# A spectral mixing kernel with a gated projection behind it: the first entry's opening regrouped, and loads, first steps and last steps reordered

## The chip, the core and the metric

The kernel runs on one core of a Trainium2 chip. The metric is the device time of one launch in microseconds, taken over several runs, of which the median is given. The engines of the core are named as the profile names them: PE (matmul; PEld is its weight load), DVE (vector), ACT (scalar activation), POOL (general purpose) and SP (which here only issues DMAs). SP, ACT and POOL each feed a queue of DMAs, and the same 16 DMA engines serve all of them.

## What is computed

`x` holds 8 entries of 3136 positions and 256 channels. Each entry goes through a real FFT along its positions, a product with a complex filter, and the inverse FFT. The 25088 rows that come out pass a projection to 1024 columns, a softmax times its input (SoLU), a layer norm and a projection back to 256 columns.

```python
X = np.fft.rfft(x, axis=1)
y = np.fft.irfft(X * (filt_r + 1j * filt_i)[None], n=3136, axis=1)   # per entry
h = y.reshape(-1, 256) @ w_in                                        # 25088 x 1024
e = np.exp(h - h.max(-1, keepdims=True))
solu = h * e / (e.sum(-1, keepdims=True) + 1e-9)
ln = (solu - mean) / np.sqrt(var + 1e-6) * g_ln
out = ln @ w_out                                                     # 25088 x 256
```

## The kernel before

The FFT of 3136 points is split as 49 times 64. A **first step** does the 49-point part: a matmul over the positions that are 64 apart. It uses that the input is real, and that position n and position 63 - n of a row of 64 can share a matmul (`N1` = 49, `N2` = 64, `NH` = 32, `NS` = 25 frequencies kept of the 49). A **spectrum** stage does the 64-point part (`forward`, L304), multiplies with the filter (`multiply`, L313), and does the 64-point inverse (`inverse`, L329), in 7 units of up to two pairs of frequencies (`NP` = 13 pairs, `self.units`, L194). A **last step** (`back`, L389 for entry 0, `back_halves`, L361 for the others) does the 49-point inverse and leaves `y`, channels on partitions, as the stationary operand for the projection.

Between the steps the data must change its partition axis, and before this change every entry does that through DRAM: the first step's rows are stored to `d1` and fetched as `t2`, the spectrum's rows are stored to `d2` and fetched as `t4`.

**The opening** (L402 to L604) is written out by hand for entry 0, and each engine and queue runs its part in that order. It loads `x` in eight pieces of four positions (`fetch_x`, L504: one half on SP's queue, the mirrored half on POOL's), runs eight times two matmuls with the table `wf_t` as stationary operand (L226), copies them out on ACT (L228), and stores them to `d1` (L230) or, for the first 16 positions, copies them from SBUF to SBUF (L559). Rows of warming matmuls (`idle`, L532) fill PE's waits. The tables of the spectrum (`load_tables`, L465) come on POOL's queue and, for the last five pairs, on SP's. After the spectrum, eight fetches of two DMAs each (`fetch_first_back`, L347: 96 rows and 4 rows, in pairs) bring `t4`, 14 warming matmuls fill the round trip, and 16 groups of four matmuls write `y`. The projection weights arrive as 64-bit floats, eight pieces of 512 KB (`load_words`, L409, on POOL's queue), and are converted by DVE, ACT and POOL (`load_float64`, L416). The order of the conversions is `convert(0)`, `(1)` before the spectrum and `(2)` to `(7)` behind it. `fetch_second` (L460) brings six of the eight pieces of entry 1's `x` on SP's queue.

**The steps.** The rest is one loop over 196 blocks of 128 rows and 9 steps that drain it (`step`, L948). Two blocks form a pair with 7 matmul products for the first projection (`product`, L715) and 7 for the second (`project`, L834), which runs four pairs behind. A step also carries pieces of the next entries' transforms; `PLAN` (L37) says in which step each piece runs. Lists by step (`top`, `early`, `middle`, `late`, `stores`, `loads`, `spectrum_loads`) hold these jobs. For entry 1 the spectrum's units run from step 4 on, and their fetches (L915) are issued on SP's queue at the end of the step two before. In the last steps `regroup` (L790) turns blocks by eight SP DMAs, `deviations` (L802) and `regroup_deviations` (L812) send the layer norm's factors through DRAM with one and four SP DMAs, and `store_out` (L863) stores the result with two.

A matmul of 32-bit floats appears in the trace as two records. Up to eight DMAs that SP and ACT issued are under way at a time: a ninth waits until the eighth before it has landed.

Of the kernel before, what the change touches and what calls it, by code (L numbers as in the profile page):

```python
# [49 lines left out]
def dft_tables():  # L50
# [39 lines left out]
    return wf.reshape(NR, NK).astype(f32), wq.reshape(P, 2, 64).astype(f32), \  # L90
# [4 lines left out]
def kernel(  # L95
# [11 lines left out]
    wf_host, wq_host, wi_host, wb_host, de_host = dft_tables()  # L107
# [76 lines left out]
    class Spectrum:  # L184
# [5 lines left out]
        def __init__(self, e, pools, load, load_de):  # L190
            self.e, self.pools = e, pools
            self.load, self.load_de = load, load_de
            self.spare = {}
            self.units = [(i, min(2, NP - i)) for i in range(0, NP, 2)]  # L194
# [117 lines left out]

        def multiply(self, i, part, add=nc.vector.tensor_tensor):  # L313
# [15 lines left out]
        def inverse(self, i, pss):  # L329
            de, prods = self.des.pop(i), self.prods.pop(i)  # L330
            for r in range(2):
                for u in range(self.shape(i)[0]):
                    rows = slice(NQ * u, NQ * u + NQ)
                    self.product(i, pss[u][NQ * r:NQ * r + NQ], lambda v: de[rows, v, 1, r, :],
                                 prods[r][rows])
# [11 lines left out]
    def fetch_first_back(ch):  # L347
        by_16((nc.sync.dma_start, nc.sync.dma_start), t4s[0, ch],
              d2[0].rearrange("s (a n) c -> (s a) n c", a=4)[:, NCH * ch:NCH * ch + NCH, :])
# [52 lines left out]
    with ExitStack() as st:  # L402
        fpool = pool("fp", 1, stack=st)
        pools = {name: pool(name + "0", bufs, stack=st)
                 for name, bufs in (("r", 1), ("t2", 1), ("p", 2), ("g", 2))}
# [3 lines left out]
        def load_words(src, n):  # L409
            raw = wpool.tile([P, 512, 2], I32, name=f"raw_{n}", tag="raw")  # L410
            nc.gpsimd.dma_start(
# [48 lines left out]
        def fetch_second():  # L460
            for i in range(6):
                second.fetch_x(i, [lambda out, in_: nc.sync.dma_start(out=out, in_=in_)] * 2,
                               spare_piece(i))

        def load_tables(i0, n, dma):  # L465
            de = fpool.tile([P, n, 2, 2, NQ], FP32, name=f"de_{i0}", tag=f"de{i0}")
            dma(out=de, in_=de_dram[i0:i0 + n].rearrange("i p k u q -> p i (k u q)"))
            f = fpool.tile([P, n, 2, C], FP32, name=f"f_{i0}", tag=f"f{i0}")
# [26 lines left out]
        def begin(j):  # L495
            raws[j] = load_words(weights[j][1], j)

# [4 lines left out]
        rows_x = pools["r"].tile([P, NH, C], FP32, name="x_0", tag="r")  # L502

        def fetch_x(h, n0, n, r0, rows, dma):  # L504

            first, step = (n0, C) if h == 0 else (N2 - 1 - n0, -C)
            dma(out=rows_x[N1 * h + r0:N1 * h + r0 + rows, n0:n0 + n],
                in_=bass.AP(tensor=x.tensor, offset=x[0].offset + r0 * N2 * C + first * C,
                            ap=[[N2 * C, rows], [step, n], [1, C]]))

        st.enter_context(tc.manual_schedule())
        nc.sync.dma_start(out=wf_t, in_=wf_dram)
        pieces = NH // NCH

        fetch_x(0, 0, NCH, 0, N1 - 1, nc.sync.dma_start)
        fetch_x(0, 0, NH, N1 - 1, 1, nc.sync.dma_start)
        for i in range(pieces):
            if i:
                fetch_x(0, NCH * i, NCH, 0, N1 - 1, nc.sync.dma_start)
            fetch_x(1, NCH * i, NCH, 0, N1, nc.gpsimd.dma_start)  # L520
            if i in (4, 7):
                begin(i // 7)
        load_tables(0, 4, nc.gpsimd.dma_start)
        load_tables(4, 4, nc.gpsimd.dma_start)
        for i in range(pieces):
            sp.xs[i] = rows_x[:, NCH * i:NCH * i + NCH]

            sp.first(i, (0, 1), ps_h.tile([P, 2, 512], FP32, name=f"pa_0_{i}", tag="h"),
                     nc.scalar.copy, sp.xs[i][0:NK])
            sp.store_first(i, 0, lambda out, in_: by_16((nc.scalar.dma_start, nc.sync.dma_start), out, in_))  # L530
# [10 lines left out]
        idle_row(8, "idle")  # L541
# [5 lines left out]
        for j in range(2):  # L547
            convert(j)
# [51 lines left out]
        for j in (5, 6, 7):  # L600
            convert(j)
# [483 lines left out]
```

## Time and profile before

| | |
|---|---|
| time, median of 3 runs | 1637.28 us (1636.35 to 1648.25) |
| the profiled execution | 1626.78 us, its span 1624.9 us |
| PE busy | 1550.2 us, 95% of the span |
| PEld busy | 1047.4 us, 64% |
| DVE busy | 1305.4 us, 80% |
| POOL busy | 1163.8 us, 72% |
| ACT busy | 902.8 us, 56% |
| DMA moved | 312.13 MB, mean 192 GB/s |
| queue q1 (SP) | 306260 packets, 169.81 MB, 40.7% of 16 engines |
| mean granted PE clock | 0.989 |

Busy shares are means over stages with different limits. In the middle of the kernel PE hardly ever stops; what happens in the first 215 us and in the last 45 us has to be read from those stretches by themselves. The profiled execution is 10.5 us below the median of the three runs, which were other launches; a sum made in the profile is a difference that is then set against the median.

### The profile page before, as it was taken

Reading aid. Unit: us, or ns where it says so; the run is one execution under the profiler, and the core shown is the slowest. Engines: PE = TensorE matmul, PEld = TensorE weight load, DVE = VectorE, ACT = ScalarE, POOL = GpSimd, SP = SyncE. Lnnn points to the kernel's source line nnn. Section 1 sums busy time; section 2 is a strip of 40 time slices with the busy share of each in tenths; the row PEclk is TensorE's granted clock in tenths of the full one; section 3 lists DMA queues with packets and bytes.
Section 4 is the critical chain, followed back from the end, with each engine's and each line's share of the span. In section 5 each row is a group of like instructions: output and inputs, shape, how many; then the busy total and the mean of one; then the engine's idle time right before and its main releaser. Section 6 shows DMA issues by size and latency. Waiting matters only on the chain.

```text
span 1624.9 us, 36998 instructions
## 1 busy us (share of the span) xinstructions
PE 1550.2 (95%) x12710; PEld 1047.4 (64%) x12710; DVE 1305.4 (80%) x2630; ACT 902.8 (56%) x1772; POOL 1163.8 (72%) x1328
## 2 busy tenths in 40 slices
PE   5798889999999999999999999999999999999997
PEld 2353356666766677666766676666777777777766
DVE  1686777998889989888999779887888777777772
ACT  2144455466565656566656655565556666665662
POOL 4445887778777877697688867788667767677774
PEclk8999899999999999999999999999999999999999
DMA  9888778877788778866787677866885554444443
GB/s 270 241 267 258 224 198 238 228 197 200 203 240 235 202 189 248 231 191 170 215 249 203 186 179 213 241 175 161 225 231 152 126 136 121 104 111 105 109 109 101
DMA packets 377805, 312.13 MB, mean 192 GB/s; under 512 B 63322, under 2 KB 343395, under 8 KB 377619
## 3 DMA queue, kind: packets, MB, share of 16 engines
q1 hardware_dynamic: 306260, 169.81, 40.7%
q0 software_dynamic: 34464, 101.68, 20.8%
q10 hardware_dynamic: 36896, 38.28, 7.9%
q8 instruction: 103, 1.69, 0.5%
q14 instruction: 82, 0.67, 0.1%
HBM read 124.86 MB, written 81.50 MB: 127 GB/s over the span
## 4 chain that ended last, share of the span: by engine, by line
PE 42%; DMA 3%; DVE 2%; issue 1%; POOL 1%; SPq 1%; ACT 0%; DVEq 0%; POOLq 0%; ACTq 0%
PE o L844 20%; PE m L723 18%; PE py L372 1%; PE pa L269 1%; PE pc L301 1%; PE pb L301 1%; DMA solu_t<-turn 1%; DMA out_dram<-ot 0%; DMA x<-in_x_dram 0%; DMA t<-d 0%; POOL u L702 0%; DMA rows<-rs 0%; DVE h L771 0%; DVE h L747 0%; SPq L816 0%
## 5 line engine op out<-in xcount | busy, mean ns | idle before, releaser
L844 PEld LDWEIGHTS o<-w_out_sb,solu_t 128*128 128x128 f32 x3136 | 381.6, 192 | 48.7 <-issue 43.0
L844 PE MATMUL o<-w_out_sb,solu_t 128*128 128x128 f32 x3136 | 400.9, 276 | 2.9 <-DVE ot L860 2.5
L723 PE MATMUL m<-w_in_sb,s 128*128 128x512 f32 x784 | 398.2, 609 | 5.1 <-DVE rsum L766 3.3
L844 PEld LDWEIGHTS o<-w_out_sb,u 128*128 128x128 f32 x2352 | 308.0, 192 | 146.4 <-issue 105.2
L844 PE MATMUL o<-w_out_sb,u 128*128 128x128 f32 x2352 | 312.0, 276 | 9.2 <-ACT ot L856 8.6
L723 PE MATMUL m<-w_in_sb,y 128*128 128x512 f32 x588 | 308.8, 608 | 8.5 <-DVE nmax L747 5.5
L771 DVE SCALAR_TENSOR_TENSOR h<-e,rsum,h 128x1024 f32<-128x1024 f32 x196 | 302.9, 1546 | 6.9
L733 ACT COPY h<-m 128x512 f32<-128x512 f32 x294 | 172.9, 588 | 241.0 <-PE m L723 217.1
L702 POOL TENSOR_TENSOR u<-solu_t 128x512 f32<-128x512 f32 x98 | 133.4, 1362 | 228.0 <-DMA solu_t<-turn 140.0
L856 ACT ACTIVATE ot<-o,rs_t 128x128 f32<-128x128 f32 x392 | 143.5, 366 | 261.1 <-PE o L844 240.1
L779 ACT ACTIVATE h<-h,nmu 128x1024 f32<-128x1024 f32 x196 | 225.0, 1148 | 51.9 <-DVE turn L787 51.4
L787 DVE STREAM_TRANSPOSE turn<-h 128x1024 f32<-128x1024 f32 x196 | 243.1, 1240 | 3.2
L747 DVE CUSTOM_DVE_ANT_0 h<-m,h 128x512 f32<-128x512 f32 x196 | 133.8, 683 | 132.3 <-ACT h L733 92.8
L755 ACT ACTIVATE e<-h,nmax 128x1024 f32<-128x1024 f32 x196 | 225.1, 1148 | 12.1 <-DVE h L771 11.8
L702 POOL TENSOR_TENSOR u<-solu_t,u 128x512 f32<-128x512 f32 x98 | 150.9, 1540 | 91.2 <-PE o L844 87.2
L723 PEld LDWEIGHTS m<-w_in_sb,s 128*128 128x128 f32 x784 | 128.8, 192 | 93.4 <-issue 84.0
L723 PEld LDWEIGHTS m<-w_in_sb,y 128*128 128x128 f32 x588 | 95.7, 191 | 108.4 <-issue 50.3
L860 DVE SCALAR_TENSOR_TENSOR ot<-o,rs_t,ot 128x128 f32<-128x128 f32 x294 | 101.9, 347 | 78.0 <-ACT ot L856 59.2
L702 POOL TENSOR_TENSOR u<-u,solu_t 128x512 f32<-128x512 f32 x98 | 162.4, 1657 | 0.9
L702 POOL TENSOR_TENSOR solu_t<-solu_t,solu_t 128x512 f32<-128x512 f32 x98 | 153.1, 1562 | 7.7
L702 POOL TENSOR_TENSOR s<-y 128x128 f32<-128x128 f32 x196 | 100.8, 514 | 0.4
L372 PEld LDWEIGHTS py<-wb_t,t 50*64 50x64 f32 x3584 | 58.0, 135 | 43.7 <-issue 22.0
(114 smaller groups left out, 1956.0 us busy)
## 6 DMA issues: line engine op xcount, KB each, us to landing
solu_t<-turn SPq DMA_DIRECT2D x784, 128.0 KB
out_dram<-ot SPq DMA_DIRECT2D x196, 128.0 KB
t<-d POOLq DMA_DIRECT2D x112, 200.0 KB, 6.2
d<-x POOLq DMA_DIRECT2D x100, 200.0 KB, 5.3
f<-f_dram POOLq DMA_DIRECT2D x39, 512.0 KB, 6.9
d<-g POOLq DMA_DIRECT2D x39, 512.0 KB, 4.8
t<-d ACTq DMA_DIRECT2D x36, 512.0 KB
x<-in_x_dram SPq DMA_DIRECT2D x112, 98.0 KB
```

Of the source, the lines that this page charges most:

```text
L372: nc.tensor.matmul(out=views[g][64 * h:64 * h + 64, cb, i, :], lhsT=t4[rows, i, c0:c0 + 64], rhs=wb_t[rows, 0:N1], start=True, stop=True)
L702: nc.gpsimd.tensor_tensor(out=out, in0=in0, in1=in1, op=op)
L723: nc.tensor.matmul(out=ms[j, bank], lhsT=lhsT, rhs=w_in_sb[:, w, :], start=m in (1, 2, 7), stop=True, skip_group_check=True)
L733: nc.scalar.copy(out=h_half(k, i), in_=ms[j, 0])
L747: nc.vector.tensor_tensor_reduce(out=h_half(k, i), in0=ms[j, bank], in1=h_half(*kept), scale=1.0, scalar=sofar, op0=ALU.add, op1=ALU.min, ...
L755: nc.scalar.activation(out=e, in_=hs[k], func=AFT.Exp, bias=nmaxs.pop(k)[:, 1:2], scale=-1.0, accum_out=esum)
L771: nc.vector.scalar_tensor_tensor(out=solu, in0=e, scalar=rsum, in1=solu, op0=ALU.mult, op1=ALU.mult, accum_out=nmu)
L779: nc.scalar.activation(out=solu, in_=solu, func=AFT.Square, bias=nmu, scale=-float(DFF), accum_out=variances[g][:, i:i + 1])
L787: nc.vector.transpose(out=turns[g][:, :, i, :], in_=solus[k].rearrange("p (f j) -> p f j", j=32))
L844: nc.tensor.matmul(out=pos[p, bank], lhsT=lhs[:, f, :], rhs=w[:, f, :], start=f == 0 and m in (1, 2, 7), stop=True, skip_group_check=True)
L856: nc.scalar.activation(out=out_half(p, *to)[0], in_=pos[p, 0], func=AFT.Copy, scale=rs)
L860: nc.vector.scalar_tensor_tensor(out=ot, in0=pos[p, bank], scalar=rs, in1=out_half(p, *kept)[0], op0=ALU.mult, op1=ALU.add)
```

## The change

It does this:

- Entry 0's `x` is loaded in two channel halves on two groups of 49 partitions (512-byte rows) on SP's and ACT's queues. Positions n and 63 - n are added and subtracted on DVE and POOL into `sums_x`, which lies in `y`. Then `sums_x` is the stationary operand: for each of 128 channels, two halves and two parts, a matmul of 49 by 64 by 25 with the small table `wx_t`, in seven groups of up to 20 channels, each copied out by ACT into `rows_x` with positions on partitions. `d1` and `t2` are not used for entry 0, nor are the SBUF-to-SBUF copies.
- `forward_whole` takes the place of `forward` for entry 0: matmuls over 128 partitions with a table (`de0`) half as large again.
- The tables come on SP's queue behind `x`. Weight pieces 0 to 3 stay on POOL's queue, 4 to 7 go to SP's, behind the fetches of `t4`. `convert(2)` moves ahead of the spectrum, `convert(3)` right behind it.
- Both sums of `multiply` run on POOL for entry 0 (one did before), and the warming matmul in each unit goes.
- `fetch_first_back` issues all eight 96-row parts, then all eight 4-row parts.
- Entry 1's spectrum fetches for steps 8, 10 and 12 move to ACT's queue and to the middle of the step two before.
- One part of the output weights' preparation moves from step 3 to step 2.
- In step 196 the exponential comes behind a projection and its copy. In step 198 the last group's factors go on POOL's queue at once.

```diff
-    def fetch_first_back(ch):
-        by_16((nc.sync.dma_start, nc.sync.dma_start), t4s[0, ch],
-              d2[0].rearrange("s (a n) c -> (s a) n c", a=4)[:, NCH * ch:NCH * ch + NCH, :])
+    def fetch_first_back(ch, part):
+        rows = (slice(0, 96), slice(96, NK))[part]
+        nc.sync.dma_start(out=t4s[0, ch][rows], in_=d2[0].rearrange("s (a n) c -> (s a) n c", a=4)[
+            rows, NCH * ch:NCH * ch + NCH, :])
...
+        def forward_whole(self, i, pss):
+            de, i0 = self.des[i], self.units[i][0]
+            for v in range(self.units[i][1]):
+                for r in range(2):
+                    for u in range(self.shape(i)[0]):
+                        nc.tensor.matmul(out=pss[r][NQ * u:NQ * u + NQ, v, :], lhsT=de[:, v, r, u, :],
+                                         rhs=self.turned[:, 2 * (i0 + v) + u, :], start=True, stop=True)
...
+        for i in range(4):
+            (nc.vector, nc.gpsimd)[i % 2].memset(x_q[32:64, :, quarter * i:quarter * i + quarter, :], 0.0)
+        for i in range(4):
+            for h in range(2):
+                fetch_x(0, h, quarter * i, quarter, 0, N1 - 1, nc.sync.dma_start)
+                fetch_x(1, h, quarter * i, quarter, 0, N1 - 1, nc.scalar.dma_start)
+            if i == 0:
+                for h in range(2):
+                    fetch_x(0, h, 0, NH, N1 - 1, 1, nc.sync.dma_start)
+                    fetch_x(1, h, 0, NH, N1 - 1, 1, nc.scalar.dma_start)
...
+        for i0, n in ((0, 4), (4, 4), (8, NP - 8)):
+            load_tables(i0, n, nc.sync.dma_start)
...
+        for i in range(4):
+            mirror(i, 0, nc.vector)
+            mirror(i, 1, nc.gpsimd if i % 2 else nc.vector)
+            if i == 1:
+                begin(0)
+            if i == 3:
+                for n in range(8):
+                    nc.tensor.matmul(out=ps_t.tile([P, 512], FP32, name=f"warm_{n}", tag="t"),
+                                     lhsT=sums_x[both, :, 0, 16], rhs=sums_x[both, 0:64, 0, 16:24],
+                                     start=True, stop=True)
+                for j in (1, 2, 3):
+                    begin(j)
+        for c0 in range(0, P, 20):
+            n = min(20, P - c0)
+            ps = ps_h.tile([P, 2, 512], FP32, name=f"pa_0_{c0}", tag="h")
+            for k in range(n):
+                for g in range(2):
+                    for part in range(2):
+                        rows = slice(64 * g, 64 * g + N1)
+                        nc.tensor.matmul(
+                            out=ps[64 * part:64 * part + 64, g, NS * k:NS * k + NS],
+                            lhsT=sums_x[rows, c0 + k, :, :].rearrange("p j m -> p (j m)"),
+                            rhs=wx_t[rows, part, 0:NS], start=True, stop=True)
+            nc.scalar.copy(
+                out=rows_x[:, 0:NS, :].rearrange("p s (g c) -> p g s c", g=2)[:, :, :, c0:c0 + n],
+                in_=ps[:, :, 0:NS * n].rearrange("p g (k s) -> p g s k", s=NS))
+            nc.tensor.matmul(out=ps_t.tile([P, 512], FP32, name=f"keep_{c0}", tag="t"),
+                             lhsT=sums_x[both, :, 0, 16], rhs=sums_x[both, 0:64, 0, 16:24],
+                             start=True, stop=True)
...
-            sp.multiply(i, 0, nc.vector.tensor_tensor)
+            sp.multiply(i, 0, nc.gpsimd.tensor_tensor)
             sp.multiply(i, 1, nc.gpsimd.tensor_tensor)
...
-            idle(pss[0])
...
-        for ch in range(pieces):
-            fetch_first_back(ch)
-        fetch_second()
+        for part in range(2):
+            for ch in range(pieces):
+                fetch_first_back(ch, part)
+        for j in (4, 5):
+            begin(j, nc.sync.dma_start)
+        fetch_second(0, 3)
+        for j in (6, 7):
+            begin(j, nc.sync.dma_start)
+        fetch_second(3, 6)
...
-            dma = nc.sync.dma_start if e == 1 else nc.scalar.dma_start
-            fetches = ahead(t, 2) if e == 1 else spectrum_loads[t - 2]
+            dma = nc.sync.dma_start if e == 1 and t < 8 else nc.scalar.dma_start
+            fetches = ahead(t, 2) if e == 1 and t < 8 else spectrum_loads[t - 2]
...
-            if 2 <= k < blocks + 2:
+            if 2 <= k < blocks:
                 exponential(k - 2)
             if proj:
                 project(p, 5)
                 keep_out(p, 1, (0, 1))
+            if blocks <= k < blocks + 2:
+                exponential(k - 2)
...
+            if j - 3 == pairs - 2:
+                deviations(j - 3, nc.gpsimd.dma_start)
             if 0 <= j - 4 < pairs:
                 project_sums(j - 4, 1)
-            if 0 <= j - 3 < pairs:
-                deviations(j - 3)
+            if j - 3 == pairs - 2:
+                regroup_deviations((j - 3) // 2, nc.gpsimd.dma_start)
+            elif 0 <= j - 3 < pairs:
+                deviations(j - 3, nc.sync.dma_start)
...
-        if k in (0, 1, 3, 4, 5, 6, 7):
-            prepare_w_out(k - (k > 2))
+        if k in (0, 1, 2, 4, 5, 6, 7):
+            prepare_w_out(k - (k > 3))
```

## The prediction

> **What bounds the kernel now.** I read the page's slices, then the busy time by stage. The columns are the stage, its length, then busy time (instructions) of PE, PEld, DVE, ACT and POOL, the granted clock, the DMA share and GB/s.
>
> ```profile
> core 0: us, PE busy (x) PEld busy (x) DVE busy (x) ACT busy (x) POOL busy (x), PEclk, DMA share, GB/s
> 0.00:10.00 10.00, 0.04 (x1) 0.04 (x1) 0.06 (x1) 0.03 (x1) 6.30 (x12) 1.00 0.80 167
> 10.00:29.00 19.00, 17.26 (x32) 6.24 (x32) 7.38 (x16) 9.35 (x9) 6.91 (x12) 1.00 1.04 317
> 29.00:50.00 21.00, 13.15 (x39) 5.21 (x43) 0.20 (x1) 1.19 (x2) 10.04 (x13) 0.76 0.89 227
> 50.00:80.00 30.00, 22.84 (x198) 10.68 (x189) 24.15 (x40) 6.44 (x12) 14.15 (x16) 0.89 0.90 265
> 80.00:92.20 12.20, 12.20 (x30) 5.43 (x29) 11.86 (x17) 1.63 (x3) 6.09 (x5) 1.00 0.80 240
> 92.20:106.50 14.30, 14.30 (x130) 14.28 (x128) 13.96 (x24) 7.29 (x15) 3.07 (x2) 1.00 0.81 227
> 106.50:133.50 27.00, 24.49 (x81) 10.72 (x80) 12.65 (x35) 11.60 (x20) 16.11 (x27) 1.00 0.85 298
> 133.50:215.00 81.50, 65.51 (x341) 28.61 (x340) 63.09 (x116) 39.94 (x73) 59.42 (x66) 0.90 0.80 235
> 215.00:1580.00 1365.00, 1349.61 (x11625) 937.24 (x11624) 1158.44 (x2354) 811.75 (x1609) 1020.41 (x1161) 1.00 0.69 186
> 1580.00:1625.00 45.00, 30.83 (x255) 28.94 (x253) 13.58 (x31) 13.58 (x31) 21.29 (x17) 0.99 0.40 104
> ```
>
> From 215 to 1580 us PE is 99% busy and the change leaves that work alone. It can gain only ahead of 106.5 us (the opening, until the first product), in the next 108 us (18 us without PE work), and in the last 45. The opening is a chain: first step until 29, the turn through DRAM until 50, spectrum until 79.9 (end of the last inverse), store and fetch until 92.2 under warming matmuls, last step until 106.5. DMA is near full through all of it.
>
> The timeline of PE shows the shape that the change multiplies, a burst of the later entries' last step, 50 rows, 64 columns loaded, 49 moved:
>
> ```profile
> 256.53 1.08 PE L372 MATMUL py<-wb_t,t 50*64 50x49 f32 x58 [0.37 <-DMA t<-d]
> 257.40 0.39 PE L301 MATMUL pb<-t,de 64*64 64x256 f32 x1
> 257.41 0.25 PE L372 MATMUL py<-wb_t,t 50*64 50x49 f32 x2
> ```
>
> 58 records start in 0.88 us, 15.2 ns each, four quarters of the array in turn.
>
> SP's timeline shows how `t4` arrives; the first of these fetches started at 86.62, and eight went out by 89.66:
>
> ```profile
> 91.33 0.30 SPq L181 DMA_DIRECT2D t<-d  x1
> 93.86 0.30 SPq L181 DMA_DIRECT2D t<-d  x1
> 95.47 0.30 SPq L181 DMA_DIRECT2D t<-d  x1
> 97.04 0.30 SPq L181 DMA_DIRECT2D t<-d  x1
> ```
>
> Each of these waits until the 96-row fetch four pairs earlier has landed: 4.7 us after the first issue, then 2.5, 1.6, 1.6 us apart, in order of issue. From the waits of PE between 106 and 215 us, the two longest:
>
> ```profile
> PE pb L301 <- DMA y<-d: 3.9, 1, 3.9
> PE pb L301 <- DMA x<-in_x_dram: 2.9, 1, 2.9
> ```
>
> They stand at 206.6 and 184.7 us, before the forward steps of entry 1 whose fetches SP issued only at 198.6 and 174.7, behind eight regrouping DMAs. The chain of waits at the end, at SP:
>
> ```profile
> 1600.37 1.88 SPq L816 DMA_DIRECT2D rs_t<-rows  x4
> 1602.35 5.36 SPq L799 DMA_DIRECT2D solu_t<-turn  x8
> ```
>
> **x.** 6272 rows of 512 B, 3.2 MB, and 0.5 MB of weights beside them. By the first stage's row 1.67 MB move in 10 us; the other 2.0 MB take 6.5 to 9 us at 317 to 227 GB/s, so 16.5 to 19. Packets are shorter now: SP's queue averages 40.7% x 16 x 1624.9 / 306260 = 34.5 ns for 554 B, ACT's 55.7 ns for 1037 B. 6272 of them on 16 engines are 13.5 or 21.8 us, so 16 to 24.3 from a start at 2.5. I take 18.5, near SP's row, whose packets are mostly this size. The memsets hold SP's half until about 3 us (2048 elements; a 128-element one took 0.17 us), its single rows until 5.5; ACT's half covers that. Without the cover: 3 us.
>
> **Mirrors.** DVE's sum of 512 elements starts every 0.61 us, POOL's takes 1.27. Behind the last quarter lie one of 1024 on each: POOL's 2.5 counts. All sums at 21.
>
> **Warming.** 16 records took 10.4 us from cold (34 to 45 us, clock 0.70). They start at 15.5, if they wait for their own quarter, or at 21: end 26 to 31.4. I take 28.5.
>
> **First step.** 512 matmuls, 1024 records x 15.2 ns = 15.6 us, plus seven warming pairs at 2 x 0.44 = 6.1 us: 50.2. The seven ACT copies (1000 elements; 1024 took 1.01) lie beside PE but the last, 0.5. The array may be kept less busy by 25 columns moved in place of 49: from 12 us (loads half hidden) to 34.6 us (each load's 135 ns over four quarters); I keep the row. [...]
>
> **Spectrum.** First forward: 16 records, two column halves, 0.215 each, 1.9 us: multiply starts at 52.6 (before: 50.15). Per unit DVE has four operations instead of five (4 x 0.61 = 2.4), POOL two sums (2.7 with gaps), PE forward 1.95 and inverse 1.1: 3.1, PE is next. 1.3 + 6 x 3.1 + 1.6 for the half unit, and 1 of the 2.6 us that POOL spends on four table DMAs: 22.5. Last inverse at 75.1 against 79.9: -4.8. The stage before held a wait of 4.8 us for `y<-d`; it is gone. If column halves do not overlap, forward costs 3.4, a unit 4.5: +8.4. The missing warming pair is covered as PE has 3.1 of every 3.1 us.
>
> **Turn and last step.** Store to fetch was 6.7 us with weights on the queues; a 128 KB store on POOL's queue lands in 3.2 us, plus 1.7 for copy and issue: 5, fetches from 80.1. Now the eight 96-row parts go first. Part 4 of a piece waits for its own piece's counter and then stands behind seven large ones, and every matmul needs both. Landings came in order of issue, so PE starts when all 3.15 MB are there. At 1.6 us each: 2 + 12.8 = 14.8 us; at the second stage's 317 GB/s: 2 + 9.9 = 11.9. If the small parts overtake, 4.6. I take 11.9, as eight large ones are now in flight with no weights beside them: start at 92.0, before 92.2. [...] PE idles 4.6 us behind its warming row and starts slower; the cold row above lost 3.5 us on 16 records (10.4 against 6.9): I take 2. First product at 108.3: **+1.8 us**.
>
> **Weights and entry 1.** SP's queue behind `t4` carries 2.1 MB of weights and 1.2 MB of `x`: at 240 GB/s the last weights land some 14 us behind `t4`, at 106, and two conversions of 4.6 us (eight DVE rows of 0.42 to 0.69) follow the last two: DVE is free near 114, before 113.3. Steps 0 and 1 (106.5 to 133.5) are PE's: 24.5 of 27 us, DVE 12.65, so 14 us of idle DVE cover it. Cover gone: 3 us. Filter stores, fetches and `convert` stand in the same order otherwise: 0.
>
> **Steps 2 to 14.** ACT issues the two late fetches some 9 us sooner, ahead of SP's regrouping. ACT may stand until a counter is free, with its copies and exponentials behind; entries 2 to 7 do so already. 6.9 us of PE wait go; DVE (63 of 81.5) and POOL's sums are next, so not all: 0 to -6.9, I take **-4.8**. The weight step from step 3 to 2: 2.5 us of DVE into idle time, 0 (± 1).
>
> **End.** SP loses four issues, 1.88 us, on the chain. POOL takes five (0.55 each) and waits for the first to land, ahead of its sums for pair 96; those were waited for from 1599.7. The exponential frees the PE copy 1.2 us sooner (PE stood 2.36 us there). 0 to -3.1: **-2.5**.
>
> Sum: 1.8 - 4.8 - 2.5 = -5.5: 1626.78 becomes 1621.3, and against the median 1637.3 - 5.5 = 1631.8.
>
> **Rivals.** *The opening does what it could* (0.20): warming starts at 15.5, small parts overtake, so PE starts behind its warming row: last inverse 72.6, last step 84.9, first product at 99.2, -7.3; with -6.9 and -3.1: 1620. For it: two moves of 3.28 MB gone, 0.85 MB of larger tables added, 5.7 MB less at 227 to 317 GB/s. Against: landings in order. *The small matmuls do not overlap* (0.12, of which 0.10 past the point below): each record then pays for its load; at 34 ns +19 us, 1651, at 135 ns +123 us. It is slower by over 1% beyond 15.2 + (16.4 + 5.5) / 1.024 = 36.6 ns. Against: the burst above. *The later gains do not come* (0.18): DVE and POOL bind in steps 4 to 14, POOL waits for its factors in the end: 1639, and 1642 with `t4` at 1.6 us. Forecast: 0.50.
>
> 1% is 16.4 us, about what a measurement can tell. Faster needs all of the first rival: 0.15. Slower needs the second: 0.10. Within: 0.75. Low end 1617 (first rival, 12 us first step), high end 1648 (`t4` at 1.6 us, `x` at 24.3, nothing later).
>
> **What would show it.** Sums at 21 and first-step records 15 ns apart; last inverse near 75; PE standing before `py` until the eighth large fetch has landed, near 92; first product near 108; no wait before entry 1's forward at steps 8 and 10; the last regrouping 2 us sooner. An `x` that lands past 24, a unit over 4 us, or `py` beginning right behind the warming row would each make it wrong.

## The result, and the profile after

The changed kernel takes 1686.16 us (median of 4 runs, 1683.59 to 1687.36) where the kernel before takes 1637.82 (median of 4, 1636.35 to 1648.25): ratio 1.0276, 95% interval 1.0237 to 1.0314 (the two medians by themselves give 1.0295). The forecast was about 1632, within 1% of no change. The profiled execution is the fastest of the four, 1683.59 us, span 1681.8 against 1624.9 before: 56.9 us more.

The stages of the changed kernel, cut where its own work changes (same columns as before: stage, length, busy time and instructions of PE, PEld, DVE, ACT and POOL, granted clock, DMA share, GB/s):

```profile
core 0: us, PE busy (x) PEld busy (x) DVE busy (x) ACT busy (x) POOL busy (x), PEclk, DMA share, GB/s
...
29.00:70.70 41.70, 36.94 (x1037) 28.42 (x1036) 4.62 (x10) 7.24 (x7) 0.00 (x0) 0.60 0.45 130
70.70:80.70 10.00, 8.49 (x55) 4.31 (x50) 7.19 (x7) 2.15 (x4) 6.96 (x5) 0.79 0.00 0
80.70:103.20 22.50, 18.13 (x152) 9.83 (x152) 18.29 (x33) 6.44 (x12) 20.30 (x19) 0.85 0.37 123
103.20:120.70 17.50, 12.31 (x31) 5.28 (x29) 5.03 (x9) 1.06 (x2) 2.58 (x2) 0.96 0.81 225
120.70:148.10 27.40, 27.40 (x129) 27.40 (x129) 2.65 (x6) 7.29 (x15) 0.00 (x0) 0.50 0.78 260
148.10:243.40 95.30, 69.71 (x300) 27.51 (x300) 70.69 (x139) 41.18 (x72) 60.90 (x77) 0.91 0.63 182
243.40:1632.20 1388.80, 1367.64 (x11730) 947.87 (x11729) 1170.89 (x2380) 822.62 (x1628) 1041.86 (x1178) 1.00 0.69 187
1632.20:1681.80 49.60, 34.74 (x266) 32.16 (x264) 16.10 (x34) 13.84 (x31) 24.87 (x23) 0.94 0.37 96
```

The rows are the first step, the way to the first spectral product, the spectrum, the fetch of the last step's rows, the last step, the steps until the first matmul of the second projection, the middle, and the end. The loss is ahead of the middle: the first projection product starts at 148.1 us (106.5 before, +41.6), and the second projection 95.3 us behind it (86.0 before, +9.3). The middle and the end are 3.0 us longer each. The clock column shows what the sum priced at nothing in the first step and at 2 us in the last: 0.60 in the first step, 0.50 for the whole last step, where PE is busy in every microsecond.

PE's timeline in the first step (start, duration, line, operation, shape, number of records; in brackets the idle time before and what ended it):

```profile
28.99 2.53 PE L588 MATMUL pa<-wx_t,y 49*64 49x25 f32 x160
31.45 1.24 PE L595 MATMUL keep<-y 113*128 113x512 f32 x2
32.62 0.88 PE L588 MATMUL pa<-wx_t,y 49*64 49x25 f32 x45
36.37 2.62 PE L588 MATMUL pa<-wx_t,y 49*64 49x25 f32 x115 [2.87 <-issue]
38.92 2.08 PE L595 MATMUL keep<-y 113*128 113x512 f32 x2
40.93 4.03 PE L588 MATMUL pa<-wx_t,y 49*64 49x25 f32 x139
46.85 0.84 PE L588 MATMUL pa<-wx_t,y 49*64 49x25 f32 x21 [1.89 <-issue]
47.62 2.08 PE L595 MATMUL keep<-y 113*128 113x512 f32 x2
49.63 4.48 PE L588 MATMUL pa<-wx_t,y 49*64 49x25 f32 x160
```

The first group is as forecast: 160 records until the next start at 31.45, 15.4 ns each, and a warming pair of 1.24 us. Then PE stops twice with nothing that the profile shows to wait for ("issue"). From 37.3 us on the clock is 0.50: a pair takes 2.08 us and a group 4.4, and both stay there to the end of the step at 70.7, long after the stops are over.

The last step's rows, at SP and at PE (the first fence is SP's timeline, the second PE's):

```profile
105.93 15.15 SPq L369 DMA_DIRECT2D t<-d  x16
```

```profile
103.21 12.28 PE L601 MATMUL idler<-f,de 128*128 128x512 f32 x28
120.69 27.60 PE L416 MATMUL py<-wi_t,t 100*128 100x98 f32 x128 [5.19 <-DMA t<-d]
```

The warming row ends at 115.5. PE stands 5.2 us, until 14.8 us after the first fetch, and the 128 records then take 27.6 us. What PE stands for are the first piece's four rows. SP issued them at 111.0, once that piece's 96 rows had landed, and they landed at 120.55, between the seventh and the eighth of the 96-row parts (119.2 and 120.8); the last four rows landed at 124.4, under PE's work. The same 128 records took 14.43 us before, right behind the same warming row:

```profile
92.21 14.43 PE L395 MATMUL py<-wi_t,t 100*128 100x98 f32 x128
```

PE's waits from 148 to 260 us, the three longest:

```profile
PE m L781 <- POOL s L760: 11.4, 1, 11.4
PE m L781 <- DVE nmax L805: 5.0, 3, 2.2
PE m L781 <- DVE rsum L824: 4.0, 2, 2.5
```

The two waits for entry 1's fetches, 3.9 and 2.9 us, are gone as forecast, but an 11.4 us wait for POOL's sums stands in step 0. At the end SP's last regrouping is no longer preceded by the four small fetches, and takes longer itself (6.55 us of issues, 5.36 before):

```profile
1652.10 1.30 SPq L926 DMA_DIRECT2D out_dram<-ot  x2
1653.51 6.55 SPq L857 DMA_DIRECT2D solu_t<-turn  x8
```

### The profile page after: what moved, and what is told of

Read it like the earlier page. It is cut to its first block, busy times and chain, and to the rows that moved or that the text cites. A ratio compares the mean times of both kernels' runs of the same rounds, so it can differ in the third digit from the quotient of the medians.

```text
span 1681.8 us, 38933 instructions
## 1 busy us (share of the span) xinstructions
PE 1584.2 (94%) x13702; PEld 1088.0 (65%) x13702; DVE 1317.0 (78%) x2631; ACT 901.8 (54%) x1771; POOL 1169.0 (70%) x1314
## 4 chain that ended last, share of the span: by engine, by line
PE 66%; DMA 13%; DVE 8%; issue 6%; POOL 3%; SPq 2%; ACT 1%; ACTq 0%; DVEq 0%; POOLq 0%
PE o L902 28%; PE m L781 27%; DMA solu_t<-turn 4%; PE py L393 3%; DMA x<-in_x_dram 3%; PE pc L312 2%; PE pa L280 2%; DMA out_dram<-ot 2%; PE py L416 2%; PE pb L312 2%; DVE turn L845 1%; DMA rs_t<-rows 1%; DVE h L829 1%; DMA t<-d 1%; SPq L857 1%
## 5 line engine op out<-in xcount | busy, mean ns | idle before, releaser
L781 PE MATMUL m<-w_in_sb,s 128*128 128x512 f32 x784 | 397.0, 607 | 21.4 <-POOL s L760 11.4
L829 DVE SCALAR_TENSOR_TENSOR h<-e,rsum,h 128x1024 f32<-128x1024 f32 x196 | 298.6, 1523 | 6.9
L813 ACT ACTIVATE e<-h,nmax 128x1024 f32<-128x1024 f32 x196 | 225.1, 1149 | 11.1 <-DVE h L829 10.5
L781 PEld LDWEIGHTS m<-w_in_sb,y 128*128 128x128 f32 x588 | 96.3, 191 | 110.3 <-issue 52.5
L393 PEld LDWEIGHTS py<-wb_t,t 50*64 50x64 f32 x3584 | 57.6, 134 | 42.9 <-issue 21.7
```

The lines of the kernel that those rows point to most:

```text
L393: nc.tensor.matmul(out=views[g][64 * h:64 * h + 64, cb, i, :], lhsT=t4[rows, i, c0:c0 + 64], rhs=wb_t[rows, 0:N1], start=True, stop=True)
L781: nc.tensor.matmul(out=ms[j, bank], lhsT=lhsT, rhs=w_in_sb[:, w, :], start=m in (1, 2, 7), stop=True, skip_group_check=True)
L813: nc.scalar.activation(out=e, in_=hs[k], func=AFT.Exp, bias=nmaxs.pop(k)[:, 1:2], scale=-1.0, accum_out=esum)
L829: nc.vector.scalar_tensor_tensor(out=solu, in0=e, scalar=rsum, in1=solu, op0=ALU.mult, op1=ALU.mult, accum_out=nmu)
```

## The experiments

Twelve kernels ran. How to read them: the runs of the kernel before on one chip lie between 1624.6 and 1645.6 us, and the middle (first second-projection product to last first-projection product), the same work in every kernel, takes 1384.8 to 1395.0 us in the profiles here. An end time of one execution is thus good to some 10 us, and the places of the first product and of the first second-projection product ("first projection") are read instead. All but 7 and 8, which are the kernel before with a part of the change, in us:

| kernel | first product | first projection | span | time |
|---|---|---|---|---|
| before | 106.5 | 192.5 | 1624.9 | 1626.78 |
| the change | 148.1 | 243.4 | 1681.8 | 1683.59 |
| 1 fetches in pairs | 127.7 | 231.8 | 1667.0 | 1668.81 |
| 2 longer warming row | 137.3 | 233.5 | 1666.4 | 1668.14 |
| 3 no warming pairs | 143.5 | 242.9 | 1674.9 | 1676.70 |
| 4 late loads | 139.4 | 236.8 | 1671.6 | 1673.40 |
| 5 conversions without ACT | 142.4 | 239.4 | 1684.2 | 1685.96 |
| 6 weights early | 149.4 | 231.6 | 1665.3 | 1667.07 |
| 9 half the instructions | 129.7 | 225.8 | 1670.8 | 1672.62 |
| 10 all, three pairs | 111.5 | 205.2 | 1645.7 | 1647.50 |
| 11 all, no pairs | 102.5 | 196.2 | 1626.4 | 1628.77 |
| 12 all, stores early | 106.2 | 192.8 | 1624.2 | 1626.11 |

### 1 and 2: idle time or late rows in the last step

Experiment 1 undoes the order of the fetches; experiment 2 leaves it and lengthens the warming row.

```diff
-        for part in range(2):
-            for ch in range(pieces):
+        for ch in range(pieces):
+            for part in range(2):
                 fetch_first_back(ch, part)
```

> The changed kernel, with the fetches of the last step's rows back in pairs (96 rows and 4 rows of one piece, then the next piece). Theory (the small parts behind eight large ones let PE fall idle for 5.2 us, and the idle time halves the clock of all that follows until the first product): PE starts the last step right behind the warming row at 115.5 us instead of 120.7, the clock stays at 1.00, the step takes 14.4 us as before the change instead of 27.6, the first product stands near 130 instead of 148.1, and the profiled execution takes about 1665 instead of 1683.6. Rival 1 (the clock falls in this step anyway): it starts near 115.5 but takes 27.6 us, first product near 143, 1678. Rival 2 (the bandwidth, not the order, sets the start): start near 120.7, nothing gained, 1683.

```diff
-        idle_row(14, "idler")
+        idle_row(22, "idler")
```

> The changed kernel, with 22 warming matmuls in place of 14 ahead of the last step; the fetches are left as they are. Each takes 0.88 us, so the row ends at 122.5 us, behind the landing of all rows (120.7). Theory (idle time halves the clock): no idle time, clock 1.00, the step takes 14.4 us, first product near 137 instead of 148.1 although it starts 1.8 us later, and the time is about 1672.5 instead of 1683.6. Rival (the late rows are the loss, the clock would be low anyway): first product near 150, 1685.5.

PE's timelines, experiment 1 and then experiment 2:

```profile
101.34 12.28 PE L601 MATMUL idler<-f,de 128*128 128x512 f32 x28
113.46 14.43 PE L416 MATMUL py<-wi_t,t 100*128 100x98 f32 x128
```

```profile
104.07 19.15 PE L601 MATMUL idler<-f,de 128*128 128x512 f32 x44
123.06 14.43 PE L416 MATMUL py<-wi_t,t 100*128 100x98 f32 x128
```

Both take 14.43 us as before the change. Experiment 2 starts the step 2.4 us later than the changed kernel and has it done 10.8 us sooner: the idle time, through the clock, was the loss, and the late rows by themselves only 5.2 us. Of the 20.4 us that experiment 1 gains at the first product (some 2 of them from shorter stops in its first step, which have nothing to do with the fetches), 11.6 reach the first projection; the rest goes into step 0, where the weights come as late as before (experiment 6).

### 3 and 4: what halves the clock in the first step

Experiment 3 leaves out the seven pairs (the `keep` matmuls, L595).

> The changed kernel without the seven warming pairs inside the first step. Theory (the pairs do not hold the clock, which is at 0.50 from 37.7 us on with them): the groups of 160 records follow each other at 4.41 us, five pairs of 2.08 us and two of some 1.2 us are saved, the first step ends near 58 instead of 70.7, everything behind it comes some 12 us sooner, time about 1671. Rival (the pairs keep the clock from falling sooner, or the issue of instructions is the limit and fills the gap): the first step is saved less than 5 us, time 1679 or more.

The step ends at 63.9 instead of 70.7, not at 58, as the stops grow from 4.8 to 7.7 us: PE's timeline.

```profile
29.61 3.22 PE L588 MATMUL pa<-wx_t,y 49*64 49x25 f32 x207
37.18 3.62 PE L588 MATMUL pa<-wx_t,y 49*64 49x25 f32 x128 [4.34 <-issue]
44.20 19.67 PE L588 MATMUL pa<-wx_t,y 49*64 49x25 f32 x689 [3.40 <-issue]
```

So of the 11.2 us that six of the pairs held up to there 6.8 were gained, between theory and rival, and only 0.5 us was left at the first projection. The fence shows more: the stops stand behind record 207 and record 335. In the changed kernel, its pairs counted, they stand behind 160 + 2 + 45 = 207 and 207 + 115 + 2 + 139 = 463. All are 207 plus a multiple of 128; the author's reading is that PE's instructions come in blocks of 128 records.

Experiment 4 empties the DMA engines during the step.

```diff
-        for i0, n in ((0, 4), (4, 4), (8, NP - 8)):
-            load_tables(i0, n, nc.sync.dma_start)
+        load_tables(0, 4, nc.sync.dma_start)
...
-                for j in (1, 2, 3):
-                    begin(j)
...
+            if c0 == 60:
+                load_tables(4, 4, nc.scalar.dma_start)
+            if c0 == 80:
+                load_tables(8, NP - 8, nc.scalar.dma_start)
+            if c0 == 120:
+                for j in (1, 2, 3):
+                    begin(j, nc.scalar.dma_start)
...
-        for j in range(3):
-            convert(j)
+        convert(0)
...
-        convert(3)
+        for j in (1, 2, 3):
+            convert(j)
```

> The changed kernel, with the tables and filter rows of pairs 4 to 12 issued by ACT behind its copies of the fourth and fifth group of the first step, and the weight quarters 1 to 3 behind the last copy; quarters 1 to 3 are converted behind the spectrum instead of ahead of it. So few transfers are in flight in the first step. Theory (PE's two stops of 3.0 and 2.0 us with nothing to wait for are its instructions, fetched through DMA engines that the loads keep full, and the first stop is what halves the clock): no stops, clock 1.00, groups of 2.5 us and pairs of 1.2, the first step ends near 53 instead of 70.7 and the multiplications begin near 57 instead of 80.7 (6 us of that from the conversions that no longer stand ahead of them); time about 1660. Rival (the small matmuls cannot hold the clock): no stops, but the clock falls to 0.50 some 4 us into the step all the same, the first step ends near 66, the multiplications begin near 70, time about 1672.

PE's timeline, and the DMA queues between 30 and 50 us (packets, MB, share of 16 engines):

```profile
37.05 0.41 PE L585 MATMUL pa<-wx_t,y 49*64 49x25 f32 x11
37.76 2.06 PE L585 MATMUL pa<-wx_t,y 49*64 49x25 f32 x128 [0.30 <-issue]
41.76 0.54 PE L585 MATMUL pa<-wx_t,y 49*64 49x25 f32 x21 [1.94 <-issue]
42.23 2.01 PE L592 MATMUL keep<-y 113*128 113x512 f32 x2
```

```profile
q10 hardware_dynamic: 23, 0.04, 2.3%
q8 instruction: 5, 0.08, 1.8%
```

The stops shrink from 4.8 to 2.2 us but do not vanish, with almost nothing in flight but the instructions: five packets in 20 us, 16 KB each. In windows of half a microsecond they stand at 31.5, 35.0, 39.0, 42.5 and 47.0 us, one in 3.5 to 4.5 us, and PE goes on some 2.5 us after each that it waited for. At 15.4 ns a block of 128 records is used up in 2.0 us. The small matmuls held a clock of 1.00 for 12 us; it fell to 0.50 at 42.6, 2.7 us after the 1.94 us stop begins, and stayed there. The step ends at 65.3, near the rival's 66, but the rival's reason does not hold: the fall comes behind a stop here, and so does each of the 15 falls in the traces of the kernel before and of the change (the last section has the count). With the conversions out of the way the multiplications start at 70.5, 5.2 us behind the end of the step instead of 10.0.

### 5: the conversions ahead of the spectrum

```diff
-            load_float64(weights[j][0], raws.pop(j), negate=j < 4, share=j < 4,
+            load_float64(weights[j][0], raws.pop(j), negate=j < 4, share=j == 3,
```

> The changed kernel, with weight quarters 0 to 2 converted by VectorE and POOL alone (ACT's multiplication and POOL's that hang on it are done by VectorE, as for quarters 4 to 7). Theory (ACT's three multiplications stand in its queue behind the seven copies of the first step, so the third conversion on VectorE waits 39 us for a buffer and the first spectral multiplication waits behind it): the conversions end within the first step, the multiplications begin near 75 instead of 80.7, right behind the first forward, and the time is about 1678 instead of 1683.6. Rival (the units would wait for something else there, such as POOL's sums or the half clock of the first forwards): the multiplications begin less than 2 us sooner, or the last inverse does not come sooner, 1682 or more.

In the changed kernel DVE's timeline has this, the end of the second conversion and the third:

```profile
33.89 0.42 DVE L444 TENSOR_SCALAR raw<-raw 128x512 int32<-128x512 int32 x1
73.34 0.43 DVE L446 TENSOR_SCALAR power<-raw 128x512 int32<-128x512 int32 x1 [39.03 <-POOL raw L464]
```

In experiment 5 the third conversion is done by 41 us and the first spectral product starts at 75.02 instead of 80.74. Of these 5.7 us 1.3 come from the first step, which ended at 69.4 by shorter stops; behind the step the product starts after 5.6 us instead of 10.0, and the 4.4 us between are the conversions'. The first product comes 5.7 us sooner, the first projection 4.0. The end does not show it: this execution's middle is the longest of all, 1395.0 us. The theory holds at its place; its worth in the time was not shown by this run.

### 6: the late weights

```diff
+        for j in (4, 5, 6, 7):
+            begin(j, nc.sync.dma_start)

         def start(i):
...
-        for j in (4, 5):
-            begin(j, nc.sync.dma_start)
-        fetch_second(0, 3)
-        for j in (6, 7):
-            begin(j, nc.sync.dma_start)
-        fetch_second(3, 6)
+        fetch_second(0, 6)
```

> The changed kernel, with the fetches of weight quarters 4 to 7 in SP's queue ahead of the spectrum (they wait there only for their buffers) instead of behind the sixteen fetches of the last step's rows; VectorE's conversions then stand whole ahead of step 0's work, as before the change. Theory (the late weights put conversions 5 to 7 behind step 0's reduction on VectorE, and POOL's sums for the next products behind them): PE's wait of 11.4 us for POOL's sums in step 0 is gone, the first projection comes 11 us sooner (181 instead of 192.5), the time is about 1672. Rival (another wait is next: entry 1's rows, or steps 0 to 8 are bound by VectorE and POOL): the first projection comes less than 5 us sooner, time 1679 or more.

The 192.5 in this text is the place of the first projection in the kernel before; in the changed kernel it is 243.4. There DVE's and POOL's timelines show the theory's chain: the conversion of weight piece 4 stands still for 23 us until the first product's `finish` has run, and POOL's sums come behind the conversions that follow (the first two lines are DVE's, the last is POOL's).

```profile
127.69 0.42 DVE L457 TENSOR_SCALAR w_out_sb<-raw 128x512 int32<-128x512 int32 x1
151.08 0.69 DVE L805 CUSTOM_DVE_ANT_0 h<-m,h 128x512 f32<-128x512 f32 x1 [22.97 <-ACT h L791]
164.56 0.64 POOL L760 TENSOR_TENSOR s<-y 128x128 f32<-128x128 f32 x1
```

In experiment 6 the 11.4 us wait is gone, and the first projection comes 82.2 us behind the first product instead of 95.3 (86.0 before the change): 13.1 us, 11.8 by the place of the first projection. The theory holds.

### 7 and 8: the end and the steps by themselves

Both are the kernel before with a part of the change. Experiment 7 takes the four hunks on `deviations`, `regroup_deviations` and the exponential:

```diff
-            if 2 <= k < blocks + 2:
+            if 2 <= k < blocks:
                 exponential(k - 2)
...
+            if blocks <= k < blocks + 2:
+                exponential(k - 2)
...
+            if j - 3 == pairs - 2:
+                deviations(j - 3, nc.gpsimd.dma_start)
...
+            if j - 3 == pairs - 2:
+                regroup_deviations((j - 3) // 2, nc.gpsimd.dma_start)
```

> The kernel before, with the last steps alone reordered as the change does it (the exponential behind the projection's first copy, the deviations of pair 96 on POOL's queue ahead of its sums). The prediction: -2.5 us (0 to -3.1). Theory now, from the changed kernel's tail of 49.6 us against 46.6: POOL waits for its own transfers ahead of its sums, PE waits for the sums, +3 us. Third possibility: both are in the noise, within 1 us of no change.

Ratio 1.0002, interval 0.9971 to 1.0033: neither the -2.5 nor the +3 us can be told from nothing. SP's last regrouping does start sooner, 21.6 us behind the last first-projection product instead of 24.0, but POOL's last sums, which wait for it, start 32.0 us behind that product instead of 31.3. The eight transfers took longer by at least as much as they began sooner.

Experiment 8 takes the two hunks on entry 1's fetches and on `prepare_w_out`:

```diff
-            dma = nc.sync.dma_start if e == 1 else nc.scalar.dma_start
-            fetches = ahead(t, 2) if e == 1 else spectrum_loads[t - 2]
+            dma = nc.sync.dma_start if e == 1 and t < 8 else nc.scalar.dma_start
+            fetches = ahead(t, 2) if e == 1 and t < 8 else spectrum_loads[t - 2]
...
-        if k in (0, 1, 3, 4, 5, 6, 7):
-            prepare_w_out(k - (k > 2))
+        if k in (0, 1, 2, 4, 5, 6, 7):
+            prepare_w_out(k - (k > 3))
```

> The kernel before, with the steps behind the opening alone reordered as the change does it (entry 1's last spectrum fetches on ACT's queue from step 8 on, the output weights' step 3 done in step 2). The prediction: -4.8 us (0 to -6.9), as PE's two waits of 3.9 and 2.9 us ahead of entry 1's forwards go. Theory now: the waits go but VectorE and POOL are next, -2 us or less, as the changed kernel shows 3 us more between its first projection and its last product than the kernel before. Rival: something in the steps after is late by it, +2 us or more.

Ratio 1.0023, interval 0.9996 to 1.0049, that is -0.7 to +8 us: the forecast -4.8 is excluded. PE's waits from the first product to 260 us, the four longest:

```profile
PE pa L269 <- POOL x L260: 6.2, 2, 4.3
PE m L723 <- DVE rsum L766: 5.1, 2, 2.6
PE m L723 <- DVE nmax L747: 3.1, 2, 1.6
PE pc L301 <- POOL y L324: 2.4, 1, 2.4
```

The waits for DMA are gone and POOL and DVE are later by as much: these four were 1.9, 3.3 and 1.7 us before, the last not there; 9.9 us more here against 6.8 saved.

### 9: half the instructions

One matmul makes both channel halves: 113 rows in place of twice 49, with zeros in the table outside two blocks, 50 columns in place of 25, the same values.

```diff
-                for g in range(2):
-                    for part in range(2):
-                        rows = slice(64 * g, 64 * g + N1)
-                        nc.tensor.matmul(
-                            out=ps[64 * part:64 * part + 64, g, NS * k:NS * k + NS],
-                            lhsT=sums_x[rows, c0 + k, :, :].rearrange("p j m -> p (j m)"),
-                            rhs=wx_t[rows, part, 0:NS], start=True, stop=True)
+                for part in range(2):
+                    nc.tensor.matmul(
+                        out=ps[64 * part:64 * part + 64, k // 10, 50 * (k % 10):50 * (k % 10) + 50],
+                        lhsT=sums_x[both, c0 + k, :, :].rearrange("p j m -> p (j m)"),
+                        rhs=wx_t[both, part, 0:2 * NS], start=True, stop=True)
```

> The changed kernel, with half the number of instructions in the first step: one matmul makes both channel halves of a channel pair (113 rows, 50 columns moved, a table with zeros outside the two diagonal blocks), 256 matmuls and 512 records instead of 512 and 1024; the copies read another layout, all else is left. Theory (PE's instructions come in blocks of 128 records, one every 3.5 to 4 us at best and 4 to 6.5 us beside the loads; the stop at the end of a block drops the clock): a group of 80 records takes about 2.2 us and its pair 1.24, so a block lasts 5.5 us, longer than its fetch; no stop over 1 us, the clock stays at 1.00, the first step ends near 52 instead of 70.7, the first product comes some 18 us sooner (130), time about 1666. Rival (these small matmuls cannot hold the clock, whatever their number): the clock falls to 0.50 in the step, groups and pairs take some 6.3 us, the first step ends near 70, no gain.

PE's timeline from the fourth group:

```profile
39.63 2.54 PE L587 MATMUL pa<-wx_t,y 113*64 113x50 f32 x80
42.10 1.23 PE L596 MATMUL keep<-y 113*128 113x512 f32 x2
43.26 2.54 PE L587 MATMUL pa<-wx_t,y 113*64 113x50 f32 x80
45.73 1.24 PE L596 MATMUL keep<-y 113*128 113x512 f32 x2
```

No stop, clock 1.00 from 28.7 to the end of the step at 51.7, the first product 18.4 us sooner (18 forecast). With the same loads in flight as in the changed kernel, half as many instructions left PE no stop, and the clock stayed at 1.00. The rival is refuted for these shapes. The number and the size of the matmuls changed together: 49x25 records without any stop were not run, and the 12 us of experiment 4 are the longest that they are seen to hold the clock.

### 10 to 12: the mendings together

Experiment 10 joins 9, 1 and 6, converts weights 0 to 3 without ACT ahead of the spectrum, and keeps three of the seven pairs; 11 leaves out all seven; 12 is 11 with two of the four filter stores on POOL's queue ahead of the spectrum.

> All mendings together: the first step with half the instructions and a pair of warming matmuls behind every second group only, the last step's rows fetched in pairs, weights 0 to 3 converted by VectorE and POOL within the first step, weights 4 to 7 fetched ahead of the spectrum; the end as in the change. If the parts add up: first step done near 48, last inverse near 72, the last step begins behind its warming row near 85 at full clock, first product near 100 (before the change: 106.5), first projection near 183 (192.5), time about 1620, some 8 us below the kernel before on the same chip (0.995). If the clock falls in the first step all the same: first step done near 64, first product near 116, time about 1636. If the steps after the first product wait for something else, the first projection stays at 192 or more whatever the first product does.

> The same without any warming pair in the first step. If the clock holds and the instructions keep up: 512 records at some 26 ns, the first step ends near 43, 4 us ahead of the version with three pairs, time about 1616. By the supply of instructions (4 us for 128 records at best) it cannot be faster than about 12 us behind the first 205 records, so it ends near 46 with stops, and a stop of 2 us drops the clock: then the records behind it take some 50 ns and the first step ends near 52.

> The version with all mendings and no warming pairs in the first step, and the filter rows of pairs 0 to 7 stored by POOL's queue ahead of the spectrum instead of by SP behind entry 1's rows. In the version without this, POOL's first sums for step 0's products wait until 119.3 us, while the vector ready last for them is there at 103: theory, they wait for buffers that the late filter stores still read (SP issues them at 102.5 to 109.6). Then PE's wait of 12.45 us in step 0 falls below 4 us, the first projection comes near 186 instead of 196.2 (before the change: 192.5), and the time is about 1618, some 0.5 to 1% below the kernel before (ratio 0.990 to 0.995). Rival (they wait for something else, or the two stores that stay on SP hold them as long): the wait stays near 12 us, first projection 196, ratio near 1.000.

Experiment 10 missed. The step ended at 52.5, not 48, with stops of 0.61 and 1.24 us behind records 207 and 335, the first product came at 111.5, not 100 (PE also stood 5.9 us for ACT's last copy of the spectrum), and the first projection at 205.2, not 183, with a wait of 9.4 us for POOL's sums. Experiment 11 ended the step at 48.5, between its two cases (its first 207 records took 6.27 us, 30.3 ns each, where 26 had been taken), and reached the first product at 102.5, 4 us ahead of the kernel before; then PE waited 12.45 us for POOL's sums. In experiment 12 that wait is 4.51 us, 7.9 less: 4.2 because POOL's first sums start at 115.1 instead of 119.3, and 3.7 because PE itself arrives later. The traces bear out the theory of the late filter stores. The semaphores on which POOL waited ahead of these sums came last with the landing of SP's last filter store, at 118.6 us in experiment 11 and at 114.7 in 12, although the label in the timeline names a fetch of `x`; so the two stores that stayed on SP still hold the sums. Its warming row took 14.7 us, until 82 us at a clock of 0.50 (PE had stood 1.77 us until 70.8 in the last units, and the clock fell at 72.1), and put the first product back to 106.2.

The first projection came at 192.8, not 186. Experiment 12 was timed: median 1631.33, not 1618, against 1636.68 of the kernel before on the same chip, ratio 0.9979 (0.990 to 0.995 expected), interval 0.9951 to 1.0007. It gives back the whole loss of the change, and a gain over the kernel before was not shown.

## Why the prediction was wrong

By its own steps; the first product was forecast at 108.3 and came at 148.1, and the parts of these 39.8 us are:

- **Warming**: done at 29.0, forecast 28.5 (+0.5). The mirrors took 2.47 us each on DVE, twice the 1.2 taken, and the last was done at 25.75 instead of 21; the warming row covered it.
- **First step**: 41.7 us instead of 21.7 (+20.0). This is the step that failed. "1024 records x 15.2 ns" was right for 160 records. The row that it was taken from is a burst of 58 records; it says nothing of a run of 1024, whose instructions came, by the reading above, in blocks of 128 records, one in 3.5 to 4.5 us at the best seen (experiment 4). The clock fell to 0.50 behind the first of the stops that follow, and these groups never got it back. Seven pairs at 2 x 0.44 were 7 x 2.08 us for the most part.
- **First multiply**: 10.0 us behind the first step instead of 2.4 (+7.6). "Filter stores, fetches and `convert` stand in the same order otherwise: 0" overlooked ACT's multiplications behind its seven copies, and DVE's third conversion behind them (experiment 5: 4.4 us of it). The forwards began at half clock, too.
- **Spectrum**: 22.3 us until the last inverse, forecast 22.5. Right.
- **Store to fetch**: 2.9 us, forecast 5 (-2.1). **Landing**: 14.8 us, forecast 11.9 (+2.9), the upper bound that was named. The mechanism was right in the main: the large parts landed 1.6 us apart on the mean, and a piece's four rows came behind the large parts that were issued ahead of them, so PE, which needed only the first piece's, started as the last large part landed.
- **Last step**: 27.4 us instead of 16.3 (+11.1). The penalty of 2 us for a cold start was mis-sized: it was taken from a row of 512-column matmuls, which lost only 3.5 us (10.4 for 16 records, at a mean clock of 0.70). This step of 98-column matmuls stayed at 0.50 to its end, and its 128 records took 27.60 us in place of 14.43 (experiments 1 and 2).

Behind the first product:

- **Weights and entry 1**, taken as 0: +9.3 us to the first projection. The landing was not what failed, but the order that follows from it: DVE's `finish` of step 0 stood in the middle of `convert(4)`, so conversions 5 to 7 waited for the first product instead of running under the last step, and POOL's sums waited for them (experiment 6: 13.1 us).
- **Steps 2 to 14**, -4.8: not there (experiment 8). The prediction named what would be late next, DVE and POOL, and then took most of the gain all the same.
- **End**, -2.5: not seen (experiment 7).

Of the rivals, "the small matmuls do not overlap" had the right side and the wrong mechanism: they do overlap, as the records of the first group start 15.4 ns apart while a weight load of theirs takes 135 ns on the mean. No case had the clock in it beyond those 2 us, so the range ended at 1648. The first group's 15.4 ns, over four quarters of the array in turn, bear out the row that the step was priced from (15.2 ns) in the time from start to start.

## What to carry to other kernels

Price a long run of small matmuls by the rate at which instructions arrive, not by a burst: count the records against the blocks (here 128 records, used up in 2.0 us and supplied in 3.5 to 4.5), and prefer fewer, larger matmuls even if they carry zeros (experiment 9 ended the step at 51.7 us instead of 70.7). Ask of every wait ahead of PE what the clock will be behind it, and whether the work behind it is of a kind that was seen to bring the clock back (here records of 113x50 did, in 3.41 us, and those of 49x25 and 100x98 did not, in 24 and 27.6); a longer warming row can be worth more than an earlier start (10.8 us in experiment 2). When a load is put later, look up where its consumers then stand in each engine's order, and what queues behind them.

## What the runs showed of the chip

- **Instructions.** The stops fell behind records 207, 335 or 463, pairs counted, in eight kernels with different loads, pairs and shapes (the change and experiments 3 to 6 and 10 to 12). Without loads an instruction packet came in 3.5 to 4.5 us, and the stops were 0.30 and 1.94 us (experiment 4); they were 3.4 and 4.3 us in experiment 3, with the loads in flight.
- **The clock fell after short stops, and in fixed steps.** In the traces of the kernel before and of the change the stretches at one clock, but for the last of each trace, last whole multiples of 3.41 us. Each of their 15 falls closes such a step in which PE was busy for 45% or less; none closes a step in which it was busy throughout. In the first step of experiments 4, 11, 12 and 10 the clock fell behind 3.41 us in which PE was busy for 43, 50, 59 and 64%. The 1.94 us of experiment 4 lay in one step, and PE had been busy again for 0.8 us when the clock fell at its end: PE was not idle all through it. The busy share alone does not settle it: in experiment 10 a stop of 1.24 us within one step was enough, in experiment 12 one of 1.26 us was not.
- **Some small work did not bring it back.** With PE busy all the time, 49x25 records with a pair of 512 columns in every group stayed at 0.50 for 24 us (from the end of the second stop in the changed kernel), and 100x98 records for 27.6 us, though the first held 1.00 for 12 us in experiment 4 and the second for 14.43 us in the kernel before, when they started with it. Records of 113x50 did bring it back, in one step of 3.41 us, in experiments 10, 11 and 12 (from 45.7 to 49.1, 38.2 to 41.6 and 37.9 to 41.3 us). What makes the difference between these kinds of work was not tried. Here is experiment 11 by microseconds (columns as in the stages above):

```profile
38.00:39.00 1.00, 1.00 (x30) 1.00 (x26) 0.96 (x3) 0.84 (x1) 0.00 (x0) 0.61 1.05 321
39.00:40.00 1.00, 1.00 (x26) 1.00 (x23) 0.97 (x3) 0.15 (x1) 0.00 (x0) 0.50 1.06 367
40.00:41.00 1.00, 1.00 (x24) 1.00 (x24) 1.00 (x3) 0.00 (x0) 0.44 (x1) 0.50 1.13 388
41.00:42.00 1.00, 1.00 (x30) 1.00 (x28) 1.00 (x1) 0.00 (x0) 0.96 (x1) 0.69 1.09 206
```

- **DVE beside POOL.** DVE's operations of 128x512 that took 0.43 us from 30.8 to 32.2 us in the changed kernel, with POOL idle, took 1.39 to 1.40 us between 73.8 and 78.1 us, while POOL multiplied and added.
